# Linear attention and a tanh-shrink MLP on one core: the opening reordered around the reciprocal, a split k load, paired column tiles, and later slots for batches 1 and 2

## Chip, core and metric

The kernel runs on one core of a Trainium2 chip. The metric is device time in microseconds (us) of one execution; the time before is the median of three runs, 284.05 us (283.96 to 284.33). In what follows PE is TensorE, PEld its weight loads, DVE is VectorE, ACT is ScalarE, POOL is GpSimd, SP is SyncE. POOL and SP issue the DMA transfers: POOL those that load inputs and weights, SP stores, small transfers by way of DRAM, and a transposing DMA. "L304" is line 304 of the kernel before.

## What is computed

```python
# q, k, v: (8 batches, 8 heads, 576 positions, 64); w_in: (512, 2048); w_out: (2048, 512)
phi = lambda x: np.where(x > 0, x, np.exp(x) - 1.0) + 1.0
q_p, k_p = phi(q), phi(k)
kv  = einsum('bhsd,bhse->bhde', k_p, v);   z = k_p.sum(axis=2)
num = einsum('bhsd,bhde->bhse', q_p, kv)
den = einsum('bhsd,bhd->bhs', q_p, z)[..., None] + 1e-06
x   = (num / den).transpose(0, 2, 1, 3).reshape(8 * 576, 512)
h   = x @ w_in
out = (h - tanh(h)) @ w_out            # (4608, 512), float32
```

## The kernel before, in words

**The two halves.** The attention gives x, kept transposed in SBUF as `xT` (feature pairs p = 0 to 3 of 128 rows, all 4608 tokens). The MLP runs over nine chunks c of 512 tokens. Of each chunk the first layer (products at L430, `l1mm`) makes 16 column tiles `fi` of 128 hidden features, four products each, one for each p; ACT takes tanh and DVE subtracts (`l1act` one tile, L441 and L442; `l1act2` two tiles at once, L436 and L437) into `gT`. The second layer (L451, `l2mm`) runs in 16 slots `s` of four products, and ACT evacuates its sums (`evac`, L462), SP stores them (L475). A batch has 576 tokens, so chunk c needs batches up to c; the attention of batch c+1 and c+2 is woven into chunk c by hand. The lists `s1[fi]` and `s2[s]` hold what is emitted after column tile fi of the first layer and after slot s of the second. Within one engine the instructions run in the order in which they are emitted, so a place in such a list sets a place in each engine's queue.

**PSUM.** The 8 banks of 2 KiB a partition are one tensor, `ps_all`. In chunk 0 the column tiles use banks 4, 5, 6, 7, 0, 1, 2, 3 in turn, the first four tiles banks 0 to 3; in later chunks tile fi uses bank fi mod 6, so tile 6 has to wait until tile 0's subtraction has read its bank, tile 8 until tile 2's has.

**The opening** (batch 0, before any chunk). q, k and v of batch 0 arrive in two transfers each (`load` with halves: i = 0, 1 is the half of the heads' positions on the partitions), cast to bf16. `phi_pieces` makes phi as min(exp(x), max(x,0)+1): exp on ACT (L136, L133 for the second half of k, which goes head by head), r and the min on DVE (L137/L134, L138/L135). `a_qT_pe` transposes q on PE (L166), copies on ACT (L170) and DVE (L172). `spin(n)` multiplies zeros while PE waits. `b0_z` (L252) sums k for z, `b0_zc` (L256) puts it into `kz`, `b0_kv` (L263) makes kv, `b0_kz` (L267) copies it, `a_den` (L333, L337) makes denominators in bank 4, and one reciprocal (L346) of 128x144 columns gives `rden`. `b0_num` (L273) makes the numerators, `b0_evac` (L293, ACT) takes them out. `b0_spread` (L300) spreads the first 128 columns of `rden` over all rows by 16 fp32 products into banks 4 to 7 (32 records in the trace), and `b0_scale` (L304, DVE, eight pieces) multiplies the two into `xT`. The last 16 columns go by way of DRAM (`spread_rest`, SP, L313 and L316). Then chunk 0's first four column tiles run (L686), 256 tokens at a time.

**Batches 1 and 2.** In chunk 0, slot s2[8] holds `kv1`, s2[9] denominators, numerators and `a_split` of batch 1, s2[12] `spread1` (L419, then the scales L423 on DVE), and s2[11], s2[13] and s2[15] the exp and min pieces of batch 2's q and, at s2[15], the transposing DMA of it (L155), the stores of chunk 0 (`later`) and the r pieces of k. In chunk 1, s1[8] holds `kv2`, and s1[12] the denominators of batch 2 (`a_den`: L337, L342, L346) with `a_spread`: four small DRAM writes `ds` (L366) and two broadcasts `rdb` (L369, 576 KB each), all on SP. `a_num` at s2[12] of chunk 1 makes the numerators and `num_scale` (L401, four pieces) reads `rdb`. POOL's `gate` (L447) holds the loads of batch 3 back until batch 2's transposing DMA is through.

Of the kernel before, what the change touches and what calls it, by code (L numbers as in the profile page):

```python
# [18 lines left out]
def kernel(  # L19
# [9 lines left out]
    nc = tc.nc  # L29
# [54 lines left out]
    def load(b, t, src, halves):  # L84

        x = src[b].rearrange("h (p j) d -> (h p) (j d)", j=J)
        if halves:
            for i in range(2):
                nc.gpsimd.dma_start(out=t[:, :, i].rearrange("q h j d -> q h (j d)"),  # L89
                                    in_=x.rearrange("(h i q) x -> i q h x", h=2, i=2)[i])  # L90
        else:
            nc.gpsimd.dma_start(out=t.rearrange("q h i j d -> q (h i) (j d)"),  # L92
                                in_=x.rearrange("(n q) x -> q n x", n=4))
# [50 lines left out]
    def a_kphi(b, i):  # L144
        phi(b, k_t, kp_t, "kp", i)
# [4 lines left out]
    def new_qT(b):  # L150
        qT_t[b] = work.tile([128, 2, J, 2, 64], BF16, name="qT")
# [4 lines left out]
            out=qT_t[b].rearrange("p i j g t -> p (i j) (g t)"),  # L156
            in_=qp_t[b].rearrange("p i j h d -> p (i j h d)"))

    def a_qT_pe(b, i, banks, on=None):
        if i == 0:  # L160
            new_qT(b)
        for n in range(2):
            j0, j1 = ((0, 5), (5, 9))[n]
            ps = banks().bitcast(BF16).rearrange("p (j t) -> p j t", t=128)
            for j in range(j0, j1):
                nc.tensor.transpose(ps[:, j - j0, :], qp_t[b][:, i, j].rearrange("p h d -> p (h d)"), ident)  # L166
            src = ps[:, 0:j1 - j0, :]
            dst = qT_t[b][:, i, j0:j1].rearrange("p j g t -> p j (g t)")
            if (on or "AV")[n] == "A":
                nc.scalar.copy(dst, src)  # L170
            else:
                nc.vector.tensor_copy(dst, src)  # L172

    def quads():

# [88 lines left out]
                                 v_b[0][rs, h, i, j, :], start=(j == 0), stop=(j == J - 1))  # L264

    def b0_kz(i):
        (nc.scalar.copy if i else nc.vector.tensor_copy)(kz_t[0][:, :, i, 0:64], ps_all[:, 2 * i:2 * i + 2, 0:64])  # L267

    def num_mm(b, i, bank_of):

# [57 lines left out]
    def a_den(b, bank, parts=range(4)):  # L328

        kz, qT = kz_t[b], qT_t[b]  # L330
        ps = ps_all[:, bank, 0:J * 16]
        for t in range(4) if b == 0 else ():
            nc.tensor.matmul(ps[32 * t:32 * t + 32], eps[:, 0:32], one[:, 0:J * 16], start=True, stop=False)  # L333
        for n, p in enumerate((0, 2, 1, 3)):
            if n in parts:
                for t in range(4):
                    nc.tensor.matmul(ps[32 * t:32 * t + 32], kz[:, p // 2, p % 2, 64:96],  # L337
                                     qT[:, p % 2, :, p // 2, 16 * t:16 * t + 16],
                                     start=(n == 0 and b > 0), stop=(n == NP - 1))
        if b > 0:  # L340
            den = rpool.tile([128, J * 16], F32, name="den")
            nc.vector.tensor_scalar(den, ps, 1e-6, None, ALU.add)  # L342
        else:
            den = ps
        rden = rpool.tile([128, J * 16], F32, name="rden")
        nc.vector.reciprocal(rden, den)  # L346
        rden_t[b] = rden

    def a_split(b):
# [187 lines left out]
    for f in (eq0, rq0, mq0, eq1, rq1, mq1):  # L537
        f()
    spin(18)
    a_qT_pe(0, 0, side, "AV")  # L540
    (ek0, rk0, mk0), (ek1, rk1, mk1) = (phi_pieces(0, k_t, kp_t, "kp", i, 2 * i) for i in range(2))
    for f in (ek0, rk0):
        f()
    spin(5)
    a_qT_pe(0, 1, side, "AV")
    for f in (*ek1, mk0, rk1):
        f()
    spin(6)
    b0_z(0)
    spin(3)  # L550
    for f in mk1:
        f()
    b0_zc(0)
    b0_kv(0)
    b0_z(1)
    b0_zc(1)
    b0_kz(0)
    a_den(0, 4)
    ns0 = new_ns(0)
    spread_rest(0)  # L560
    b0_num(0)
    b0_kv(1)
    b0_kz(1)
    b0_evac(0, ns0)
    b0_num(1)
    b0_evac(1, ns0)
    b0_spread((0, 2, 1, 3), 0)
    for x in range(2):
        for n, p in enumerate((0, 2, 1, 3)):
            b0_scale(p, ns0, n, 4 * x, 4 * x + 4)  # L570

    def prepare():

# [12 lines left out]
    for c in range(NC):  # L586
# [4 lines left out]
        if c == 0:  # L591
            sub = {}

            def spread1():
                a_spread_pe(1, range(NP))
                for p in range(NP):
                    a_scale(1, p, sub["ns"], p)

            def kv1():
                a_kv(1, 4)  # L600
                pss = rest_mm(0, 4, 256)
                a_kz(1, 4)
                scale_rest(0, pss)

            def num1():
                ns = sub["ns"] = new_ns(1)
                for i in (1, 0):
                    b0 = 4 + 2 * i
                    num_mm(1, i, lambda h: b0 + h)
                    nc.scalar.copy(ns[:, i::2, 0:8, :].rearrange("p a j t -> p a (j t)"), ps_all[:, b0:b0 + 2, :])  # L610

            s2[0].append(lambda: a_qphi(1, 0))
            s2[1].append(lambda: a_qphi(1, 1))
            s2[4].append(lambda: a_kphi(1, 0))
            s2[5].append(lambda: (a_qT_pe(1, 0, Banks([4, 5])), a_qT_pe(1, 1, Banks([6, 7])), a_kphi(1, 1),
                                  load_q(2), load_k(2), load_v(2)))
            s2[2].append(prepare)
            s2[8].append(kv1)
            s2[9].append(lambda: (a_den(1, 4), num1(), spread_rest(1), a_split(1)))
            s2[12].append(spread1)  # L620

            qs, ks = [], []

            def exp2(pieces, src, store, name, i):
                pieces.append(phi_pieces(2, src, store, name, i))
                pieces[i][0]()

            def rest2(f):
                f[1]()
                f[2]()  # L630

            def k2(i):
                ks.append(phi_pieces(2, k_t, kp_t, "kp", i))
                ks[i][1]()

            s2[11].append(lambda: exp2(qs, q_t, qp_t, "qp", 0))
            s2[13].append(lambda: (rest2(qs[0]), exp2(qs, q_t, qp_t, "qp", 1)))
            s2[15].append(lambda: (rest2(qs[1]), a_qT_dma(2), [f() for f in later], k2(0), k2(1)))
        elif n1 < B:
            if c == 1:  # L640
                def kv2():
                    kv_cols_mm(2, 6, 0)
                    pss = rest_mm(1, 6, 256)
                    kz_copy(2, 6, 0)
                    scale_rest(1, pss)

                s1[8].append(kv2)
            if n1 < QS:
                s1[12].append(lambda: (a_den(n1, 6), a_spread(n1)))
            else:  # L650
                if c == 2:
                    s1[2].append(lambda: (q_den(n1, 0, 0), q_den(n1, 0, 1)))
                e = 2 * (c == 2)
                s1[3 + e].append(lambda: q_den(n1, 1, 0))
                s1[5 + e].append(lambda: q_den(n1, 1, 1))
                s1[7 + e].append(lambda: q_scale(n1))
            m = 12 if c == 1 else 9
            s2[m].append(lambda: a_num(n1, n2 if n2 < B else 0))
            if n2 < B:
                s2[m + 2].append(lambda: (q_zb(n2, 4 if c == 1 else 7), q_prod(n2)))  # L660
                if c > 1:
                    s2[15].append(lambda: (q_den(n2, 0, 0), q_den(n2, 0, 1)))
# [15 lines left out]
        if c == 0:  # L678

            first = Banks([4, 5, 6, 7, 0, 1, 2, 3])  # L680
            hs = [ps_all[:, n, :] for n in range(4)]
            for x in range(2):
                xs = slice(256 * x, 256 * x + 256)
                for n, p in enumerate((0, 2, 1, 3)):
                    for fi in range(4):
                        nc.tensor.matmul(hs[fi][:, xs], w_in_sb[:, p, fi * 128:(fi + 1) * 128], xT[:, p, xs],  # L686
                                         start=(x == 0 and n == 0), stop=(x == 1 and n == 3))
            for fi in range(4):
                l1act(fi, hs[fi], gT)
        for fi in range(4 if c == 0 else 0, NF):  # L690
            h = first() if c == 0 else ps_all[:, fi % 6, :]
            if c == 2 and fi == 1:

                for two in (0, 2):
                    for f, o in ((0, ps_all[:, 0, :]), (1, h)):
                        for p in (two, two + 1):
                            l1mm(c, f, o, p, p)
            elif c != 2 or fi > 1:
                for p in range(NP):
                    l1mm(c, fi, h, p, p)  # L700
            if c == 0:
                l1act(fi, h, gT)
            elif fi % 2:
                n = fi % 6
                l1act2(fi - 1, ps_all[:, n - 1:n + 1, :], gT)
            for f in s1[fi]:
                f()
# [56 lines left out]
```

## Time and profile before

| what | value |
|---|---|
| median of three runs | 284.05 us (283.96 to 284.33) |
| the profiled execution, its own time | 284.32 us |
| its span, first to last instruction | 282.6 us |
| PE busy in the span | 277.0 us, 98% |
| DVE, ACT, POOL busy | 176.1, 145.6, 77.5 us |
| granted TensorE clock | 1.000 |
| first product of chunk 0 (L686), first of L430 | 16.82 us, 20.30 us |
| mean of one L430 product, recorded | 379 ns (they overlap; 36 of them follow each other in 7.77 us) |

A timeline line gives start, duration, engine, line, operation, output and inputs, how many instructions are merged in it, and in brackets the idle time ahead of it with what ended it. The chain of work that ended last is followed back from the last instruction, at each step to what released it. Times of a record include its way through the engine's pipeline, so records in a row overlap by some 0.07 us on DVE.

### The profile page before, as it was taken

What the parts mean: (1) busy time and instruction counts of PE and PEld (TensorE: products, weight loads), DVE (VectorE), ACT (ScalarE), POOL (GpSimd) and SP (SyncE); (2) the same over time, 40 slices, a digit from 0 to 9 for tenths busy, and PEclk for the clock granted to TensorE, in tenths of its full rate; (3) what the DMA queues carried; (4) which work ended last, traced back from release to release, by engine and by line L of the source; (5) the groups of instructions that cost most, each with busy time, mean ns of one, the idle gap of its engine ahead of it and who ended that gap; (6) DMA issues with size and microseconds to landing.
All of it is one profiled execution on the core that took longest, in us unless ns stands there. A gap on an engine that the chain in (4) does not pass through costs nothing.

```text
span 282.6 us, 5093 instructions
## 1 busy us (share of the span) xinstructions
PE 277.0 (98%) x2084; PEld 131.9 (47%) x2084; DVE 176.1 (62%) x283; ACT 145.6 (52%) x176; POOL 77.5 (27%) x69
## 2 busy tenths in 40 slices
PE   8989999999999999999999999999999999999995
PEld 3564454454444454445444444444444444444443
DVE  5859977984779773977397639764870167006600
ACT  3648647946346753566366735572651365126411
POOL 8653120430361526233614360506050000000000
PEclk9999999999999999999999999999999999999999
DMA  6999999899994399049903792252115210230032
GB/s 103 199 207 212 205 207 209 172 192 197 236 237 76 71 194 217 5 84 162 220 22 73 115 240 60 48 110 48 29 22 123 58 32 2 57 79 13 2 74 75
DMA packets 38743, 33.12 MB, mean 117 GB/s; under 512 B 16160, under 2 KB 34624, under 8 KB 38592
## 3 DMA queue, kind: packets, MB, share of 16 engines
q0 software_dynamic: 17504, 18.35, 40.1%
q1 hardware_dynamic: 21216, 14.45, 21.8%
q8 instruction: 16, 0.26, 0.3%
q14 instruction: 7, 0.06, 0.1%
HBM read 38.14 MB, written 9.46 MB: 168 GB/s over the span
## 4 chain that ended last, share of the span: by engine, by line
PE 90%; DMA 5%; POOL 1%; ACT 1%; issue 1%; SPq 0%; DVE 0%; DVEq 0%; POOLq 0%
PE ps_all L430 43%; PE ps_all L451 41%; DMA v<-in_v_dram 3%; DMA out_dram<-osb 3%; PE ps_all L184 2%; PE ps_all L273 2%; PE ps_all L686 1%; ACT osb L462 1%; SPq L475 0%; POOL kraw L89 0%; PE ps_all L337 0%; POOL qraw L89 0%; PE ps_all L300 0%; PE ps_all L166 0%; PE ps_all L263 0%
## 5 line engine op out<-in xcount | busy, mean ns | idle before, releaser
L451 PE MATMUL ps_all<-w_out_sb,gT 128*128 128x512 bf16 x560 | 124.6, 379 | 0.0
L430 PE MATMUL ps_all<-xT,w_in_sb 128*128 128x512 bf16 x560 | 122.7, 379 | 0.0
L437 DVE TENSOR_TENSOR gT<-ps_all,th 128x1024 bf16<-128x1024 f32 x64 | 77.8, 1218 | 46.4 <-ACT th L436 46.4
L436 ACT ACTIVATE th<-ps_all 128x1024 f32<-128x1024 f32 x64 | 65.5, 1024 | 46.9 <-PE ps_all L430 46.9
L430 PEld LDWEIGHTS <-w_in_sb 128*128 128x128 bf16 x560 | 54.6, 98 | 65.5
L451 PEld LDWEIGHTS <-gT 128*128 128x128 bf16 x560 | 53.8, 98 | 63.2 <-issue 0.2
L462 ACT COPY osb<-ps_all 128x512 f32<-128x512 f32 (+1 forms) x36 | 20.7, 582 | 56.4 <-PE ps_all L451 40.0
L245 POOL TENSOR_TENSOR qp<-qp,rd 128x1152 bf16<-128x1152 bf16 x10 | 21.0, 2118 | 39.1 <-issue 23.7
L231 POOL TENSOR_TENSOR pr<-qp,zb 128x1152 f32<-128x1152 bf16 x10 | 23.5, 2362 | 21.6 <-ACT zb L224 21.6
L236 DVE TENSOR_REDUCE dn<-pr 128x9 f32<-128x576 f32 x20 | 14.5, 745 | 12.2 <-POOL pr L231 12.2
L136 ACT ACTIVATE e<-qraw 128x1152 bf16<-128x1152 bf16 x16 | 18.5, 1161 | 5.4 <-DMA qraw<-in_q_dram 5.4
L136 ACT ACTIVATE e<-kraw 128x1152 bf16<-128x1152 bf16 x15 | 17.4, 1162 | 1.9 <-DMA kraw<-in_k_dram 1.9
L138 DVE TENSOR_TENSOR qp<-e,r 128x1152 bf16<-128x1152 bf16 x16 | 12.1, 759 | 4.4 <-ACT e L136 3.3
L92 POOL DMA_DIRECT2D kraw<-in_k_dram x7 | 5.4, 769 | 33.1 <-DVE r L137 17.7
L138 DVE TENSOR_TENSOR kp<-e,r 128x1152 bf16<-128x1152 bf16 x15 | 11.4, 763 | 4.4 <-ACT e L136 3.5
L441 ACT ACTIVATE th<-ps_all 128x512 f32<-128x512 f32 x16 | 9.4, 597 | 5.5 <-PE ps_all L686 3.7
L442 DVE TENSOR_TENSOR gT<-ps_all,th 128x512 bf16<-128x512 f32 x16 | 10.4, 687 | 2.7 <-ACT th L441 1.7
L532 PE MATMUL ps_all<-zero 128*128 128x512 bf16 x32 | 10.1, 475 | 1.2 <-DVE zero L485 1.2
L92 POOL DMA_DIRECT2D qraw<-in_q_dram x7 | 5.2, 741 | 16.7 <-ACT e L136 7.3
L137 DVE TENSOR_SCALAR r<-qraw 128x1152 bf16<-128x1152 bf16 x16 | 7.4, 465 | 0.4 <-DMA qraw<-in_q_dram 0.4
L460 DVE COPY osb<-ps_all 128x128 f32<-128x128 f32 x1 | 0.3, 292 | 11.6 <-DMA out_dram<-osb 11.6
L199 DVE COPY vp<-v 128x1152 bf16<-128x1152 bf16 x10 | 5.3, 525 | 3.2 <-DMA v<-in_v_dram 3.2
(105 smaller groups left out, 141.1 us busy)
## 6 DMA issues: line engine op xcount, KB each, us to landing
out_dram<-osb SPq DMA_DIRECT2D x62, 128.0 KB, 2.5
qraw<-in_q_dram POOLq DMA_DIRECT2D x7, 576.0 KB, 10.5
kraw<-in_k_dram POOLq DMA_DIRECT2D x7, 576.0 KB, 7.8
v<-in_v_dram POOLq DMA_DIRECT2D x6, 576.0 KB, 11.4
w_in_sb<-in_moe_w_in_dram POOLq DMA_DIRECT2D x3, 512.0 KB, 13.1
w_out_sb<-in_moe_w_out_dram POOLq DMA_DIRECT2D x3, 512.0 KB, 16.3
v<-in_v_dram POOLq DMA_DIRECT2D x4, 288.0 KB, 12.9
rdb<-ds SPq DMA_DIRECT2D x2, 576.0 KB
```

Of the source, the lines that this page charges most:

```text
L92: nc.gpsimd.dma_start(out=t.rearrange("q h i j d -> q (h i) (j d)"), in_=x.rearrange("(n q) x -> q n x", n=4))
L136: return (lambda: nc.scalar.activation(e, x, AF.Exp), lambda: nc.vector.tensor_scalar(r, x, 0.0, 1.0, ALU.max, ALU.add), lambda: nc.vector ...
L138: lambda: nc.vector.tensor_tensor(y, e, r, ALU.min))
L231: nc.gpsimd.tensor_mul(pr_t[b][:, i].rearrange("p j h d -> p j (h d)"), qp_t[b][:, i].rearrange("p j h d -> p j (h d)"), zb_t[b][:, i].uns ...
L236: nc.vector.tensor_reduce(dn_t[b][:, i, :, h], pr_t[b][:, i, :, h, :], mybir.AxisListType.X, ALU.add)
L245: nc.gpsimd.tensor_mul(x, x, rd[:, i].unsqueeze(2).to_broadcast([128, J * 2, D]))
L430: nc.tensor.matmul(h, w_in_sb[:, p, fi * 128:(fi + 1) * 128], xT[:, p, c * 512:(c + 1) * 512], start=(n == 0), stop=(n == NP - 1))
L436: nc.scalar.activation(th, h, AF.Tanh)
L437: nc.vector.tensor_sub(gT[:, fi:fi + 2, :], h, th)
L442: nc.vector.tensor_sub(gT[:, fi, :], h, th)
L451: nc.tensor.matmul(o, gT[:, fi, i * 128:(i + 1) * 128], w_out_sb[:, fi, :], start=(fi == 0), stop=(fi == NF - 1))
L462: nc.scalar.copy(osb[:, f0:f1], o[:, f0:f1])
```

## The change

It does these things:
- the second part of batch 0's k is loaded in two transfers, one for each head of a pair;
- in the opening the copy of the second q half on ACT comes after both exp halves of k, z(1) ahead of kv(0), `kz` of half 0 is copied by ACT and that of half 1 by DVE, two spin products fewer;
- batch 0's reciprocal is two instructions, of 128 and 16 columns; the spread comes ahead of the second numerators, the rest's DMAs behind them in emission;
- the scales and the first four column tiles go by the pairs of i = 0 first, then i = 1; two column tiles share two banks, and tanh and subtraction take two tiles at a time;
- batch 1's slots go from s2[8], [9], [12] to [9], [10], [13]; batch 2's q exp from [11], [13] to [13], [14], its min pieces all to [15];
- in chunk 1 `kv2` goes from s1[8] to [9], the denominators of batch 2 from s1[12] to [13]; column tiles 0 and 1 of chunk 1 are interleaved as those of chunk 2 were.

```diff
         if halves:
+            y = x.rearrange("(h i q) x -> i q h x", h=2, i=2)
             for i in range(2):
-                nc.gpsimd.dma_start(out=t[:, :, i].rearrange("q h j d -> q h (j d)"),
-                                    in_=x.rearrange("(h i q) x -> i q h x", h=2, i=2)[i])
+                for hs in ((0, 1), (1, 2)) if i and src is k and b == 0 else ((0, 2),):
+                    nc.gpsimd.dma_start(out=t[:, hs[0]:hs[1], i].rearrange("q h j d -> q h (j d)"),
+                                        in_=y[i, :, hs[0]:hs[1]])
...
     def b0_kz(i):
-        (nc.scalar.copy if i else nc.vector.tensor_copy)(kz_t[0][:, :, i, 0:64], ps_all[:, 2 * i:2 * i + 2, 0:64])
+        (nc.vector.tensor_copy if i else nc.scalar.copy)(kz_t[0][:, :, i, 0:64], ps_all[:, 2 * i:2 * i + 2, 0:64])
...
-        nc.vector.reciprocal(rden, den)
+        for x in (slice(0, 128), slice(128, 144)) if b == 0 else (slice(0, 144),):
+            nc.vector.reciprocal(rden[:, x], den[:, x])
...
-    spin(5)
-    a_qT_pe(0, 1, side, "AV")
-    for f in (*ek1, mk0, rk1):
+    spin(4)
+    t1a, t1v = a_qT_pe(0, 1, side)
+    for f in (t1v, *ek1, t1a, mk0, rk1, *mk1):
         f()
     spin(6)
     b0_z(0)
-    spin(3)
-    for f in mk1:
-        f()
+    spin(2)
     b0_zc(0)
+    b0_z(1)
     b0_kv(0)
-    b0_z(1)
+    b0_kz(0)
     b0_zc(1)
-    b0_kz(0)
     a_den(0, 4)
     ns0 = new_ns(0)
-    spread_rest(0)
     b0_num(0)
+    b0_evac(0, ns0)
     b0_kv(1)
     b0_kz(1)
-    b0_evac(0, ns0)
+    spread_rest(0)
+    b0_spread((0, 2, 1, 3), 0)
     b0_num(1)
     b0_evac(1, ns0)
-    b0_spread((0, 2, 1, 3), 0)
-    for x in range(2):
-        for n, p in enumerate((0, 2, 1, 3)):
-            b0_scale(p, ns0, n, 4 * x, 4 * x + 4)
+    for i in range(2):
+        for x in range(2):
+            for n, p in ((2 * i, i), (2 * i + 1, 2 + i)):
+                b0_scale(p, ns0, n, 4 * x, 4 * x + 4)
...
-            s2[8].append(kv1)
-            s2[9].append(lambda: (a_den(1, 4), num1(), spread_rest(1), a_split(1)))
-            s2[12].append(spread1)
+            s2[9].append(kv1)
+            s2[10].append(lambda: (a_den(1, 4), num1(), spread_rest(1), a_split(1)))
+            s2[13].append(spread1)
...
-            s2[11].append(lambda: exp2(qs, q_t, qp_t, "qp", 0))
-            s2[13].append(lambda: (rest2(qs[0]), exp2(qs, q_t, qp_t, "qp", 1)))
-            s2[15].append(lambda: (rest2(qs[1]), a_qT_dma(2), [f() for f in later], k2(0), k2(1)))
+            s2[13].append(lambda: exp2(qs, q_t, qp_t, "qp", 0))
+            s2[14].append(lambda: exp2(qs, q_t, qp_t, "qp", 1))
+            s2[15].append(lambda: (rest2(qs[0]), rest2(qs[1]), a_qT_dma(2), [f() for f in later], k2(0), k2(1)))
...
-                s1[8].append(kv2)
+                s1[9].append(kv2)
             if n1 < QS:
-                s1[12].append(lambda: (a_den(n1, 6), a_spread(n1)))
+                s1[13].append(lambda: (a_den(n1, 6), a_spread(n1)))
...
-            hs = [ps_all[:, n, :] for n in range(4)]
-            for x in range(2):
-                xs = slice(256 * x, 256 * x + 256)
-                for n, p in enumerate((0, 2, 1, 3)):
-                    for fi in range(4):
-                        nc.tensor.matmul(hs[fi][:, xs], w_in_sb[:, p, fi * 128:(fi + 1) * 128], xT[:, p, xs],
-                                         start=(x == 0 and n == 0), stop=(x == 1 and n == 3))
-            for fi in range(4):
-                l1act(fi, hs[fi], gT)
+            hs = [ps_all[:, fi // 2:4:2, 256 * (fi % 2):256 * (fi % 2) + 256] for fi in range(4)]
+            for i in range(2):
+                for x in range(2):
+                    xs = slice(256 * x, 256 * x + 256)
+                    for f0 in (0, 2):
+                        for p in (i, i + 2):
+                            for fi in (f0, f0 + 1):
+                                nc.tensor.matmul(hs[fi][:, x, :], w_in_sb[:, p, fi * 128:(fi + 1) * 128], xT[:, p, xs],
+                                                 start=(p == 0 and fi == f0), stop=(p == 3 and fi > f0))
+            for n in range(2):
...
-            if c == 2 and fi == 1:
+            if c in (1, 2) and fi == 1:
...
-            elif c != 2 or fi > 1:
+            elif c not in (1, 2) or fi > 1:
```

More of the change, by code (lines that the diff above doesn't have):

```diff
@@ L157, in a_qT_dma, with a_qT_pe @@
             in_=qp_t[b].rearrange("p i j h d -> p (i j h d)"))
-    def a_qT_pe(b, i, banks, on=None):
+    def a_qT_pe(b, i, banks, on="AV"):
         if i == 0:
             new_qT(b)
+        copies = []
         for n in range(2):
@@ L168, in a_qT_pe @@
             dst = qT_t[b][:, i, j0:j1].rearrange("p j g t -> p j (g t)")
[L169 to L172, printed above, removed]
+            copies.append((nc.scalar.copy if on[n] == "A" else nc.vector.tensor_copy, dst, src))
+        return [lambda f=f, d=d, x=x: f(d, x) for f, d, x in copies]
     def quads():
@@ L539 @@
     spin(18)
-    a_qT_pe(0, 0, side, "AV")
+    for f in a_qT_pe(0, 0, side):
+        f()
     (ek0, rk0, mk0), (ek1, rk1, mk1) = (phi_pieces(0, k_t, kp_t, "kp", i, 2 * i) for i in range(2))
@@ L614 @@
             s2[4].append(lambda: a_kphi(1, 0))
[L615 removed]
+            s2[5].append(lambda: ([f() for i in range(2) for f in a_qT_pe(1, i, Banks([4 + 2 * i, 5 + 2 * i]))], a_kphi(1, 1),
                                   load_q(2), load_k(2), load_v(2)))
             s2[2].append(prepare)
[L618 to L620 removed]
+            s2[9].append(kv1)
+            s2[10].append(lambda: (a_den(1, 4), num1(), spread_rest(1), a_split(1)))
+            s2[13].append(spread1)
             qs, ks = [], []
@@ L680 @@
             first = Banks([4, 5, 6, 7, 0, 1, 2, 3])
-            hs = [ps_all[:, n, :] for n in range(4)]
-            for x in range(2):
-                xs = slice(256 * x, 256 * x + 256)
-                for n, p in enumerate((0, 2, 1, 3)):
-                    for fi in range(4):
-                        nc.tensor.matmul(hs[fi][:, xs], w_in_sb[:, p, fi * 128:(fi + 1) * 128], xT[:, p, xs],
-                                         start=(x == 0 and n == 0), stop=(x == 1 and n == 3))
-            for fi in range(4):
-                l1act(fi, hs[fi], gT)
+            hs = [ps_all[:, fi // 2:4:2, 256 * (fi % 2):256 * (fi % 2) + 256] for fi in range(4)]
[8 more added lines that the diff above has]
+            for n in range(2):
+                th = mpool.tile([128, 2, 512], F32, name="th")
+                h = ps_all[:, n:4:2, :]
+                nc.scalar.activation(th, h, AF.Tanh)
+                nc.vector.tensor_sub(*(y.rearrange("p x (f t) -> p f x t", f=2) if i else
+                                       y.rearrange("p f (x t) -> p f x t", x=2)
+                                       for i, y in enumerate((gT[:, 2 * n:2 * n + 2, :], h, th))))
         for fi in range(4 if c == 0 else 0, NF):
             h = first() if c == 0 else ps_all[:, fi % 6, :]
-            if c == 2 and fi == 1:
+            if c in (1, 2) and fi == 1:
                 for two in (0, 2):
```

## The prediction

> **What bounds the kernel now.** I read the page first (busy shares, then the chain that ended last), then the chain in order of time, then the timelines of TensorE (PE), VectorE (DVE) and the DMA queue SP around the places that the change touches.
>
> ```profile
> PE 277.0 (98%) x2084; PEld 131.9 (47%) x2084; DVE 176.1 (62%) x283; ACT 145.6 (52%) x176; POOL 77.5 (27%) x69
> PE 90%; DMA 5%; POOL 1%; ACT 1%; issue 1%; SPq 0%; DVE 0%; DVEq 0%; POOLq 0%
> ```
> ```profile
> 4.80 7.41 DMA v<-in_v_dram
> ...
> 14.37 0.27 ACT kz L267
> ...
> 14.69 0.41 PE ps_all L273 x4
> 15.10 1.15 PE ps_all L300 x32
> ...
> 16.34 0.43 DVE xT L304
> ...
> 16.82 3.65 PE ps_all L686 x32
> 20.47 10.36 PE ps_all L430 x48
> ```
> TensorE is the bound: once the first real product starts at 16.82 us it is never idle for long until the stores at 269 us. So three things can move the time: when the product at 16.82 starts, TensorE's own work (the change adds and removes no product outside the opening), and new waits of TensorE later. Three spots of other engines decide those waits:
>
> ```profile
> 46.16 2.48 DVE L423 TENSOR_TENSOR xT<-ns,ps_all 128x512 bf16<-128x512 f32 x4 [1.18 <-PE ps_all L419]
> ...
> 51.76 1.22 DVE L437 TENSOR_TENSOR gT<-ps_all,th 128x1024 bf16<-128x1024 f32 x1
> ...
> 53.67 1.21 DVE L437 TENSOR_TENSOR gT<-ps_all,th 128x1024 bf16<-128x1024 f32 x1
> ```
> ```profile
> 62.60 1.05 DVE L346 RECIPROCAL rden<-den 128x144 f32<-128x144 f32 x1
> 63.57 1.16 DVE L437 TENSOR_TENSOR gT<-ps_all,th 128x1024 bf16<-128x1024 f32 x1
> ```
> ```profile
> 68.75 1.12 SPq L369 DMA_DIRECT2D rdb<-ds  x2
> ```
> ```profile
> L401 DVE TENSOR_TENSOR xT<-ps_all,rdb x4: 681/681/681, 77.3 to 79.1; 128x512 bf16<-128x512 f32 x4
> L401 DVEq EVENT_SEMAPHORE  x1: 21/21/21, 77.1 to 77.1; - x1
> ```
> Between 46.16 and 57.95 DVE has no idle row: its queue is full. And the last line shows batch 2's scale (L401) standing at 77.1 at a wait for the broadcast rdb; the landing events of the second broadcast end at 77.08. It has about 0.15 us to spare, since DVE is busy until 77.37 anyway.
>
> **The opening.** Before: both `min` halves of k (L135) end at 12.62; the second one waits for the second `Exp` half (ACT to 12.12), whose first half could start only when all of k's second part had landed (10.8). With h=0 in a transfer of its own, that first `Exp` is done before; the second runs 10.87 to 11.54 (0.67, row L133), and DVE runs r (0.45) and both halves (0.46, then 0.38 after overlap) back to back from the landing: 12.25, a gain of 0.37. The moved ACT copy t1a (0.68) then ends at 12.2, before its reader at 13.2. On PE, z(1) now goes ahead of kv(0): kv(0) (0.28 of starts) lay in the shadow of that wait and now lies on the path, so the last L337 ends at 13.45 instead of 13.68. kz of half 0 goes from DVE to ACT (0.28 to 0.27) and is done at 13.4, before num(0) needs it. Spins of zeros (two fewer matmuls) fill waits only.
>
> The reciprocal in two: the rows 128x144 (1053 ns) and 128x36 (378 ns) give 6.25 ns a column and 0.15 fixed, so 0.95 and 0.25, some 0.08 of it overlapped. It starts at 13.49 instead of 13.73 and ends at 14.62 instead of 14.79. The spread (L300) is now ahead of num(1), which held it from 14.84 to 15.03; it starts at 14.68, ends 0.35 earlier, and the first scale goes from 16.34 to 15.99, the first product from 16.82 to 16.46. Does the spread wait for both pieces? In before, the first L304 reads columns 0 to 63 of the four banks, which the spread's first four products write, yet starts after the last of the 32 at 16.25: waits go by whole PSUM banks. The spread writes the bank that both pieces read, so I take both; released by the first piece alone it would start 0.19 earlier.
>
> The Trainium skill (PSUM — Partial Sum Buffer, "PSUM bank collisions raise a hardware error") asks for guards by bank even where columns differ, so it too speaks against the split: by it the split costs about 0.1 (a second fixed cost), by column-wise guards it brings the 0.19.
>
> The L686 block: products go by pairs of i, 0.109 each. The second scale comes 0.34 after the first, two products fill 0.22, so 0.12 of wait; the evacuation of i=1 (1.03, now after num(1)) ends at 17.2, before banks 2 and 3 are needed at 17.4; i=1's scales (17.3 to 18.8) keep ahead. The full-width L430 start goes from 20.30 to 20.07: **-0.23**.
>
> The third k transfer is one more issue on POOL (0.72 by its rows), ahead of v and the weights. Their transfers are queued: issues 0.72 apart land about 1.45 apart, v issued at 4.80 lands at 12.2. So I cost the slot at nothing; without that cover v and w_in come 0.72 later. Ends: -0.5 (spread released early, k's second piece a little earlier) to +0.5 (second piece 0.7 late).
>
> The Trainium skill (DMA: Bandwidth & Descriptors, "Anatomy of one DMA — SWDGE (gpsimd) path") gives about 2.0 us fixed per transfer; paid in series this would turn -0.23 into about +1.8. The rows' 1.45 spacing shows that it is overlapped.
>
> **First four column tiles by pairs.** Two tanh of 1.02 and two subtractions of 1.22 take the place of four of 0.60 and 0.69; banks 0 to 3 are free again at 22.1 and 23.3 for products at 23.5 and later. Zero; were this late, each bank would cost its lateness.
>
> **Slots of batch 1 (0.86 us later each).** kv, den and num move with equal distance; their inputs (v of batch 1 landed by 39.6) only get older: zero. The spread L419 moves from 45.63 to 46.49 in PE's own time, so L423 starts at 47.02, not 46.16, and everything queued behind it on DVE with no idle time is 0.86 later: the four q pieces, two k pieces, and the first L437s. xT's pairs 2 and 3 are ready at 49.0 and 49.6; the interleaved first two column tiles of c=1 want them at 49.43 and 49.64: covered; without the interleave 0.35. The first L437 then ends at 53.84 (52.98+0.86), but column tile 6 wants its bank at 48.57+24x0.2158 (7.77/36, the chain's row of L430) = 53.75: wait 0.15 with 0.055 of hand-over. The second ends at 55.74, tile 8 wants its bank at 55.47+0.15: another 0.18. Together **+0.32**; ends 0 (DVE recovers) and 0.6.
>
> Also behind those q pieces: the transposing DMA (SP, 2.83) and eight stores, later by 0.86-0.23 = 0.63, and POOL's gate (L447), which holds back the loads of batch 3: its v lands at 71.1 instead of 70.5, the vp and kp pieces behind it end at 73.7, two us before PE reads them. The stores and qT's readers have over 3 us. ACT's two moved `Exp` have data (q of batch 2 landed 46.3) and free banks in time.
>
> **Slots of batch 2.** kv2 one tile later: inside slack. The denominators move from after tile 12 to after tile 13, and so behind the L437 of tiles 12/13 in DVE's queue. In PE's time the tile-13 products end at 61.75, tanh 61.8 to 62.8, L437 to 64.1, den 0.30, reciprocal to 65.4, where it was 63.65: +1.74, not one slot. With PE itself at +0.09 (-0.23+0.32) that is +1.83 for what hangs on it: the four ds writes, the wait until 68.75 for their landing, the two 576 KB broadcasts. Their data ran after v of batch 3 had landed (70.5), on an otherwise empty software queue, so they gain nothing by starting later: landing 78.9. L401 starts at 79.0 (was 77.29); its fourth piece ends 2.48 later, 81.5. PE wants pair 3 at 80.13+0.09. Wait: 81.5+0.05-80.22 = **+1.3**. Ends: 0.4, if the reciprocal moves by the slot alone (0.86); 1.6, if the stores interleave worse. Nothing gives this back: later stages are full of PE.
>
> **Sum:** -0.23+0.32+1.3 = +1.4. The profiled execution took 284.32 (span 282.6 and 1.7 around), 0.27 over the median; it would become 285.7, the median 285.45.
>
> **Rivals.**
> A, the forecast, +0.9 to +1.7. For it: the wait row at 77.1 and the queue order. 70%.
> B, the broadcast is hidden: it lands by 78.0, DVE is ready then and stage c=2 waits 0.3 or less. Sum -0.23+0.32+0.2 = +0.3, 284.35. For it: it ran beside 8 stores and a k load, so some of its 8.3 us may be contention. Against: the ds writes themselves take the 3.4 us from 64.96 at the last issue. 17%.
> C, faster: the opening gains 0.5 or more and the DVE queue does not hold PE, since the spread is released by the first piece of the reciprocal and the interleaved order hides the late scales; with both later waits at zero, -0.5 to -0.7, 283.4. It decides if the broadcast lands before 77.7. Against: the full DVE rows after 46.16. 7%.
> D, the k pieces: the extra issue delays v, w_in and what follows by its 0.72 on top of A, 286.1. 6%.
>
> **How the numbers follow.** 0.2%, 0.57 us, is about what a measurement of this kernel can tell from no change: 283.48 and 284.62 are the bounds. Faster: C and a little of B, 0.08. Same: B and A's lowest part, 0.18. Slower 0.74. The range from 284.1 to 286.0 leaves out C, half of D and B's low end; A alone is 284.95 to 285.75.
>
> **What would show it.** First L686 near 16.46 and L430 near 20.07. PE waits for L437 of about 0.15 each at tiles 6 and 8 of c=1. L346 of batch 2 near 64.4 to 65.5, after the L437 of tiles 12/13. The waits of TensorE should then list xT from the L401 line near 80 with about 1 us. Wrong if that wait is absent, or if the broadcast lands before 78.

## The result and the profile after

The changed kernel takes 286.59 us (median of 6 runs, 286.27 to 287.76); the kernel before took 284.19 beside it (6 runs, 283.96 to 284.87). The ratio is 1.0086, with a 95% interval from 1.0065 to 1.0107: slower, as forecast, but by 2.4 us where the sum had 1.4, and 0.6 above the upper end of the range. The profiled execution took 286.76 with a span of 285.0 (before 282.6), at a granted clock of 1.0 in both, so the spans can be laid side by side. One execution of the kernel before (487 us) and one of `e6_slots_pairs` (484 us) ran at 0.56 of the clock and are left out of the medians and ratios below. In line numbers, L686 of before is now L690, L430 is L432, L437 is L439, L441/L442 are L443/L444, L138 is L140, L199 is L200, L346 is L348, L401 is L403, L423 is L425, L369 is L371, L300 is L301, L184 is L185; of k's second half in the opening, r is L136 (L134) and the min L137 (L135); the pairs of the first four tiles are L695 (tanh) and L696 (subtraction).

The busy shares and the chain that ended last, page of the changed kernel:

```profile
PE 277.6 (97%) x2082; PEld 131.7 (46%) x2082; DVE 176.7 (62%) x282; ACT 145.4 (51%) x174; POOL 77.8 (27%) x70
PE 82%; DMA 8%; DVE 5%; issue 1%; ACT 1%; SPq 1%; POOL 0%; DVEq 0%; POOLq 0%
```

The busy time of every engine is the same to 0.6 us; what has changed is who ends last. TensorE's part of the chain has fallen from 90% to 82%. The chain in order of time of the same run says where the others have come in (start, duration, what):

```profile
10.82 0.65 DVE r L136
11.57 0.84 DVE kp L137 x2
13.72 1.08 DVE rden L348 x2
14.84 1.22 PE ps_all L301 x32
16.63 3.76 PE ps_all L690 x32
...
53.84 1.65 DVE kp L140
55.49 1.15 DVE gT L439
56.68 1.89 PE ps_all L432 x8
...
65.61 1.06 DVE rden L348
67.69 4.10 DMA ds<-rden
71.80 0.48 SPq L371
72.33 7.59 DMA rdb<-ds
80.01 2.50 DVE xT L403 x4
```

Before, hardly anything but TensorE stood in the chain between 16.82 and 269 us. Now there are two breaks: a piece of batch 2's k (kp, L140) that takes 1.65 us in chunk 1, and the way from batch 2's reciprocal by way of DRAM to the scales of chunk 2. The waits of TensorE name the same two (us in total, times, longest):

```profile
PE ps_all L432 <- DVE gT L439: 0.8, 1, 0.8
...
PE ps_all L432 <- DVE xT L403: 0.6, 3, 0.2
```

That view counts idle time after the modelled end of the pipeline. Measured from one product's start to the next, less the usual 0.216 us, the stalls after 16.6 us are: 0.16 at column tile 9 of chunk 0, 0.15 at tile 6 and 0.98 at tile 8 of chunk 1, and 0.41, 0.38 and 0.34 at the first products of chunk 2. With the first L432 at 20.23 instead of 20.30 this gives -0.07+0.16+0.15+0.98+1.13 = +2.35, against +2.4 between the spans; another 0.08 lies inside kv of batch 2 in chunk 1.

**The break in chunk 1.** VectorE's timeline of the changed kernel and its kp row in the kernel before, then GpSimd's of the changed kernel, then GpSimd's of the kernel before (start, duration, engine, line, operation, how many merged, idle time ahead):

```profile
47.10 2.48 DVE L425 TENSOR_TENSOR xT<-ns,ps_all 128x512 bf16<-128x512 f32 x4 [1.19 <-PE ps_all L421]
...
52.71 1.22 DVE L439 TENSOR_TENSOR gT<-ps_all,th 128x1024 bf16<-128x1024 f32 x1
53.84 1.65 DVE L140 TENSOR_TENSOR kp<-e,r 128x1152 bf16<-128x1152 bf16 x1
55.41 1.21 DVE L439 TENSOR_TENSOR gT<-ps_all,th 128x1024 bf16<-128x1024 f32 x1
```
```profile
52.90 0.85 DVE L138 TENSOR_TENSOR kp<-e,r 128x1152 bf16<-128x1152 bf16 x1
```
```profile
52.50 2.38 POOL L200 COPY vp<-v 128x1152 bf16<-128x1152 bf16 x2 [10.64 <-DMA v<-in_v_dram]
```
```profile
51.99 2.76 POOL L199 COPY vp<-v 128x1152 bf16<-128x1152 bf16 x2 [11.08 <-DMA v<-in_v_dram]
```

The same kp piece takes 0.76 us elsewhere and took 0.85 at this place before. It has two bf16 inputs in SBUF; GpSimd at that time copies v of batch 2 in two pieces. In the changed kernel the second copy runs from 53.74 to 54.88; kp starts 0.10 after the copy's start, and ends 0.61 after its end. Before, kp started at 52.90, 0.24 before the first copy's end, and again ended 0.61 after it; there kp went next, and it was the second copy that took 1.68 instead of 1.14. So the two take turns: whoever comes second stands until the other's instruction is through. The Trainium skill (SBUF — State Buffer, "Who interferes with whom") says this: a VectorE instruction with two SBUF inputs contends with a GpSimd instruction that reads SBUF, and the first to start holds the port to its end. Both orders of this pair of traces agree with it (1.65 for the one, 1.68 for the other).

**The break at chunk 2.** SP's and VectorE's timelines of the changed kernel, to be read against 68.75 (SP) and the last row here (VectorE) of the kernel before:

```profile
71.80 1.12 SPq L371 DMA_DIRECT2D rdb<-ds  x2
```
```profile
65.61 1.05 DVE L348 RECIPROCAL rden<-den 128x144 f32<-128x144 f32 x1
...
80.01 2.48 DVE L403 TENSOR_TENSOR xT<-ps_all,rdb 128x512 bf16<-128x512 f32 x4 [1.37 <-DMA rdb<-ds]
```
```profile
77.29 2.48 DVE L401 TENSOR_TENSOR xT<-ps_all,rdb 128x512 bf16<-128x512 f32 x4
```

VectorE now idles for 1.37 us until the broadcast lands. The reciprocal is 3.0 later than before: 1.3 that TensorE is late by then, and 1.7 of its own.

**The pairs.** ScalarE's timeline of the changed kernel:

```profile
19.99 1.02 ACT L695 ACTIVATE th<-ps_all 128x1024 f32<-128x1024 f32 x1 [2.57 <-PE ps_all L690]
22.37 1.02 ACT L695 ACTIVATE th<-ps_all 128x1024 f32<-128x1024 f32 x1 [1.35 <-DVE gT L696]
```

The second tanh (banks 1 and 3) waits for the first subtraction (banks 0 and 2), although they share no bank. VectorE then runs 0.95 late through chunk 0: batch 1's q pieces start at 33.05 instead of 32.10.

### The profile page after: what moved, and what is told of

It is laid out like the page before. It is cut to its first block, busy times and chain, and to the rows that moved or that the text cites. A ratio compares the mean times of both kernels' runs of the same rounds, so it can differ in the third digit from the quotient of the medians.

```text
span 285.0 us, 5087 instructions
## 1 busy us (share of the span) xinstructions
PE 277.6 (97%) x2082; PEld 131.7 (46%) x2082; DVE 176.7 (62%) x282; ACT 145.4 (51%) x174; POOL 77.8 (27%) x70
## 4 chain that ended last, share of the span: by engine, by line
PE 82%; DMA 8%; DVE 5%; issue 1%; ACT 1%; SPq 1%; POOL 0%; DVEq 0%; POOLq 0%
PE ps_all L432 40%; PE ps_all L453 35%; DMA rdb<-ds 3%; DMA out_dram<-osb 2%; DMA qraw<-in_q_dram 2%; PE ps_all L185 2%; DMA ds<-rden 1%; PE ps_all L690 1%; PE ps_all L274 1%; DVE xT L403 1%; ACT e L138 1%; DVE rden L348 1%; DVE gT L439 1%; ACT osb L464 1%; DVE kp L140 1%
## 5 line engine op out<-in xcount | busy, mean ns | idle before, releaser
L432 PE MATMUL ps_all<-xT,w_in_sb 128*128 128x512 bf16 x560 | 123.5, 379 | 1.5 <-DVE gT L439 0.8
L439 DVE TENSOR_TENSOR gT<-ps_all,th 128x1024 bf16<-128x1024 f32 x64 | 77.7, 1217 | 45.9 <-ACT th L438 45.8
L432 PEld LDWEIGHTS <-w_in_sb 128*128 128x128 bf16 x560 | 54.6, 98 | 68.0 <-issue 3.1
L138 ACT ACTIVATE e<-qraw 128x1152 bf16<-128x1152 bf16 x16 | 18.5, 1161 | 3.6 <-DMA qraw<-in_q_dram 3.6
L138 ACT ACTIVATE e<-kraw 128x1152 bf16<-128x1152 bf16 x15 | 17.4, 1162 | 1.0 <-DMA kraw<-in_k_dram 1.0
L140 DVE TENSOR_TENSOR kp<-e,r 128x1152 bf16<-128x1152 bf16 x15 | 12.2, 815 | 4.4 <-ACT e L138 3.5
L140 DVE TENSOR_TENSOR qp<-e,r 128x1152 bf16<-128x1152 bf16 x16 | 12.1, 758 | 4.4 <-ACT e L138 3.5
L444 DVE TENSOR_TENSOR gT<-ps_all,th 128x512 bf16<-128x512 f32 x12 | 7.8, 686 | 0.8
L443 ACT ACTIVATE th<-ps_all 128x512 f32<-128x512 f32 x12 | 7.2, 597 | 2.0 <-DVE gT L444 1.1
L200 DVE COPY vp<-v 128x1152 bf16<-128x1152 bf16 x10 | 5.2, 524 | 2.7 <-DMA v<-in_v_dram 2.7
```

The source lines that it names most:

```text
L138: return (lambda: nc.scalar.activation(e, x, AF.Exp), lambda: nc.vector.tensor_scalar(r, x, 0.0, 1.0, ALU.max, ALU.add), lambda: nc.vector ...
L140: lambda: nc.vector.tensor_tensor(y, e, r, ALU.min))
L432: nc.tensor.matmul(h, w_in_sb[:, p, fi * 128:(fi + 1) * 128], xT[:, p, c * 512:(c + 1) * 512], start=(n == 0), stop=(n == NP - 1))
L439: nc.vector.tensor_sub(gT[:, fi:fi + 2, :], h, th)
```

## The experiments

Every run has the kernel before beside it on the same chip, and each ratio is to it; its medians there were 284.43 (`e1` to `e4`), 284.33 (`e5` to `e8`) and 284.36 (`e9` to `e11`). The changed kernel was timed only beside the 284.19 above, so a distance from its 286.59 also holds the 0.14 to 0.24 us between those medians.

**Both sets of slots back.** `e1_slots_back`, the changed kernel with

```diff
-            s2[9].append(kv1)
+            s2[8].append(kv1)
-            s2[10].append(lambda: (a_den(1, 4), num1(), spread_rest(1), a_split(1)))
+            s2[9].append(lambda: (a_den(1, 4), num1(), spread_rest(1), a_split(1)))
-            s2[13].append(spread1)
+            s2[12].append(spread1)
...
-                s1[13].append(lambda: (a_den(n1, 6), a_spread(n1)))
+                s1[12].append(lambda: (a_den(n1, 6), a_spread(n1)))
```

and q's pieces of batch 2 and `kv2` back likewise.

> The changed kernel with the slots of batches 1 and 2 as in the kernel before; opening, pairs and interleave stay. Theory A (the time went to late queues of VectorE: 1.13 us of waits in chunk 1 and 1.13 us at the start of chunk 2): both go, 284.2 to 284.5 us. Rival B (the paired tiles and the split k load cost more than the trace's 0.16 us at tile 9, by way of VectorE being 0.95 us later in chunk 0): the time stays above 285.3.

Measured: 285.25 us, ratio 1.0029 (1.0019 to 1.0039); between the theories. The stalls at chunk 2 are gone, but 0.8 stays, and a wait has come that the changed kernel does not have:

```profile
PE ps_all L185 <- DVE kp L140: 0.5, 1, 0.5
```

That is kv of batch 1, which at its old slot meets the VectorE that the pairs have made late (0.62 from start to start, with 0.16 at tile 9 and 0.26 at tile 8 of chunk 1). So the pairs are not free; in the changed kernel the later slot of kv hides most of their cost. The old slots don't keep kp away from GpSimd's copy either: with TensorE and VectorE late by then for these reasons, kp starts at 53.84 and takes 1.65 here too.

**Only the denominators of batch 2 back.** `e2_den_back`, the changed kernel with the last two lines of the diff above alone.

> The changed kernel with batch 2's denominators back after column tile 12 of chunk 1. Theory A (the reciprocal stands behind the subtraction of tiles 12/13, everything up to the broadcast hangs on it): reciprocal 1.8 us earlier, broadcast landed by 78.2, the 1.13 us of waits at chunk 2's start gone, 1.1 us less than the changed kernel. Rival B (the broadcast lands late because its transfers collide with the stores, whenever they start): the landing moves by less than 0.9 and 0.5 us or more of wait stay.

Measured: 285.43, ratio 1.0036 (1.0025 to 1.0048), 1.16 below the changed kernel (1.4 by the distances from the kernel before, 1.0 against 2.4). The reciprocal starts at 63.68, the scales at 78.39 with no idle time ahead, and chunk 2 starts without a wait; the waits in chunk 1 stay (0.14 and 0.98). The term of batch 2's slot is shown.

**The same from the other side.** `e7_den_later_alone`, the kernel before with this one line changed the other way (s1[12] to s1[13]).

> The kernel before with one edit: the denominators and reciprocal of batch 2 in chunk 1 go from s1[12] to s1[13]. Theory A (the reciprocal then stands behind the subtraction of tiles 12 and 13, and the broadcast lands later by as much): reciprocal of batch 2 at about 64.4 instead of 62.60, the scales L401 about 1.2 to 1.8 later than 77.29, waits of TensorE in sum 0.6 to 1.3 at the start of chunk 2: 285.0 to 285.6. Theory B (it costs only on top of a chunk 1 that is late already): under 284.7.

Measured: 285.60, ratio 1.0046 (1.0030 to 1.0062), that is +1.27. VectorE's timeline of this run:

```profile
64.20 1.05 DVE L346 RECIPROCAL rden<-den 128x144 f32<-128x144 f32 x1
78.82 2.48 DVE L401 TENSOR_TENSOR xT<-ps_all,rdb 128x512 bf16<-128x512 f32 x4 [1.56 <-DMA rdb<-ds]
```

One slot later costs 1.6 us at the reciprocal, because it gets behind the subtraction of tiles 12 and 13, and 1.35 at TensorE (0.63+0.38+0.33). Theory A: the edit costs as much where chunk 1 is on time.

**The kp pieces out of the way.** `e3_kp_later`, the changed kernel with

```diff
-                s1[1 + 2 * i].append(lambda i=i: (ks[i][0](), ks[i][2]()))
+                s1[3 + 2 * i].append(lambda i=i: (ks[i][0](), ks[i][2]()))
```

> The changed kernel with batch 2's k pieces (exp and min) two column tiles later, so the subtraction of tiles 2/3 goes ahead of the first min. Theory A (the min, two bf16 operands in SBUF, was held until GpSimd's copy of v ended at 54.88, and the subtraction stood behind it): first min at its usual 0.76, wait at tile 8 gone, wait at tile 6 0.15 as before, about 1.0 us less than the changed kernel. Rival B (VectorE is slow in that stretch for another reason): the subtraction of tiles 2/3 or the min is stretched in its new place too, gain below 0.5.

Measured: 286.07 (285.34 to 287.03), ratio 1.0068 (1.0049 to 1.0088). In the profiled run, 285.34, kp starts behind both copies and takes its usual time, and the 0.98 at tile 8 is gone:

```profile
54.64 0.75 DVE L140 TENSOR_TENSOR kp<-e,r 128x1152 bf16<-128x1152 bf16 x1
```

The 1.2 at chunk 2 stays. The trace is that of theory A, but the median is only 0.5 below the changed kernel, where 1.0 was expected. The four times scatter by 1.7 us; what the longer ones met isn't shown, since only one execution was profiled.

**v's copies on VectorE.** `e4_vp_dve`, the changed kernel with

```diff
-            s1[0].append(lambda: (a_vp(2, 0, nc.gpsimd), a_vp(2, 1, nc.gpsimd),
-                                  gate(qT_t[n1]), load_k(n2), load_q(n2), load_v(n2)))
+            s1[5].append(lambda: (a_vp(2, 0), a_vp(2, 1)))
+            s1[0].append(lambda: (gate(qT_t[n1]), load_k(n2), load_q(n2), load_v(n2)))
```

> The changed kernel with batch 2's two copies of v done by VectorE after tile 5, none by GpSimd. Theory A (shared access of VectorE and GpSimd to SBUF): the first min takes 0.76 again, the wait at tile 8 falls from 0.98 to 0.18, 0.7 to 0.8 us less than the changed kernel. Rival B (the transposing DMA, issued at 52.1, slows the min): the min stays at 1.6 and the time does not fall.

Measured: 286.43, ratio 1.0070 (1.0055 to 1.0085): hardly below the changed kernel. The first kp takes 0.75 with no copy on GpSimd, and tile 8 waits only 0.08. The time goes elsewhere: kv of batch 2 now waits 0.35 for vp, and the stall at chunk 2 is 1.35, which take back 0.57 of the 0.90. In the profiled run, the slowest of the four at 286.86, the opening was also 0.6 later (first L432 at 20.84 instead of 20.23), which this edit doesn't touch. So the mechanism is confirmed and the transposing DMA is ruled out, and as a repair the edit gains little.

**The pairs in neighbouring banks.** `e5_pairs_next`, the changed kernel with

```diff
-            hs = [ps_all[:, fi // 2:4:2, 256 * (fi % 2):256 * (fi % 2) + 256] for fi in range(4)]
+            hs = [ps_all[:, fi - fi % 2:fi - fi % 2 + 2, 256 * (fi % 2):256 * (fi % 2) + 256] for fi in range(4)]
...
-                h = ps_all[:, n:4:2, :]
+                h = ps_all[:, 2 * n:2 * n + 2, :]
```

> The changed kernel with one edit: the two column tiles of a pair lie in neighbouring banks (0 and 1, then 2 and 3) and not in every second one (0 and 2, then 1 and 3). Same number and size of instructions. Theory A (the wait of ACT's second tanh for the first subtraction comes from the overlapping stretches of banks): the second tanh starts about 21.1 instead of 22.37, the second subtraction ends near 23.4 instead of 24.65, the wait of 0.16 at column tile 9 is gone, and the q pieces of batch 1 start on DVE about 1.1 earlier (near 31.9). The later waits (0.98 at tile 8 of chunk 1, 1.1 at the start of chunk 2) stay, so 0.1 to 0.3 us less than the changed kernel: 286.3 to 286.5. Theory B (the tanh waits for the banks it shares with something else, or for its buffer): the second tanh stays at 22.4 and nothing moves.

Measured: 286.52, ratio 1.0076 (1.0060 to 1.0092). The two subtractions now follow each other (21.37 to 23.73) and the wait at tile 9 is gone, so the overlap of the strided stretches made the tanh wait (whether the chip asks for that or only the program's own guards isn't shown). The total is what was expected only because its parts cancel. Products now write bank 2 earlier, while the second numerators are still being read from it, and the L690 block has 0.30 more of wait. And in chunk 1 the collision has moved to another victim, VectorE's timeline and the wait behind it:

```profile
52.14 2.72 DVE L139 TENSOR_SCALAR r<-kraw 128x1152 bf16<-128x1152 bf16 x2
```
```profile
PE ps_all L432 <- DVE gT L439: 1.9, 1, 1.9
```

GpSimd's copies started at 51.99 in this run, and both r pieces of k (one SBUF input, usually 0.45) take 1.40 behind them. TensorE waits 2.0 at tile 6, and not at all at the start of chunk 2. TensorE's lateness alone doesn't explain that, for the reciprocal hangs on it and comes 1.0 later too (66.63). But the broadcast was issued 3.7 us after the first ds write, where the other twelve profiles have 5.0 to 5.3. With 5.1 it would have landed some 1.4 later, and the stall would have been about that of the changed kernel (an estimate: the changed kernel's 8.2 from this issue to the scales puts them at 81.0 with the first product wanted at 81.36, against 80.01 and 80.35 there). What shortened the way in this run isn't shown.

**Slots back and neighbouring banks.** `e6_slots_pairs`, both edits together.

> The changed kernel with the slots of batches 1 and 2 as before, and the pairs in neighbouring banks. Theory A (the 0.9 us by which the run with the old slots alone stood over the kernel before were the pairs' 0.95 us of lateness on DVE, paid as 0.16 at tile 9, 0.62 at kv of batch 1 and 0.26 at tile 8 of chunk 1): these waits go, and the time is within 0.4 of the kernel before, 284.0 to 284.8. Theory B (the rest of the change, the opening above all, costs by itself): it stays at 285.0 or more.

Measured: 284.59, ratio 1.0008 (0.9998 to 1.0018). Without the pairs' lateness the waits at tile 9 and at kv are gone; 0.26 at tile 8 of chunk 1 (kp again 1.66) and the 0.30 in the L690 block stay. Theory A.

**The third k transfer undone.** `e8_k_two`, the changed kernel with

```diff
-                for hs in ((0, 1), (1, 2)) if i and src is k and b == 0 else ((0, 2),):
+                for hs in ((0, 2),):
```

> The changed kernel with the second part of batch 0's k in one transfer again. Theory A (the third transfer frees only one of the two exponentials, and the r that bounds the chain then runs beside POOL's next issue at 0.64 instead of 0.45): time within 0.3 of the changed kernel, first product of chunk 0 between 16.6 and 16.9. Theory B (the third transfer is what brings the opening forward): first product 0.3 or more later, 17.0 or more, and 0.3 us or more over the changed kernel. Theory C (the extra issue costs v and the weights 0.7): 0.3 us or more under it.

Measured: 286.43, ratio 1.0072 (1.0054 to 1.0090); first L690 at 16.64 (changed kernel 16.63). Theory A: within 0.2 of the changed kernel, neither gain nor cost can be seen. In this profile all of k's second part had landed at 10.19 (before 10.78), so the r piece, which ended at 11.48, set the chain even with one transfer; what the split is worth when k lands late isn't shown.

**The later slots of batch 1 alone.** `e10_b1_alone`, the kernel before with kv, denominators and spread of batch 1 one slot later and the interleave of chunk 1:

```diff
-            s2[12].append(spread1)
+            s2[13].append(spread1)
...
-            if c == 2 and fi == 1:
+            if c in (1, 2) and fi == 1:
```

> The kernel before with two edits of the change: kv, denominators and spread of batch 1 at s2[9], [10], [13], and the first two column tiles of chunk 1 interleaved. Theory A (the kp piece of DVE, 0.86 later, now arrives while POOL's second vp copy holds what both need, and takes about 1.6 us instead of 0.85): a wait of TensorE of 0.5 to 1.0 at column tile 8 of chunk 1, 0.1 to 0.2 at tile 6: 284.9 to 285.5. Theory B (the lateness on DVE passes on and no more, as the sum of the prediction had it): 0.3 in all, 284.5 to 284.75, the kp piece at 0.85 or less.

Measured: 285.39, ratio 1.0032 (1.0020 to 1.0044), +1.03. Theory A in its cause and its size, though not in its place: the scales L423 start at 46.98 (before 46.16, as forecast), and here it is the second r piece of k that meets the copies, so the wait of TensorE (1.09) is at tile 6:

```profile
51.84 1.80 DVE L137 TENSOR_SCALAR r<-kraw 128x1152 bf16<-128x1152 bf16 x2
53.56 1.21 DVE L437 TENSOR_TENSOR gT<-ps_all,th 128x1024 bf16<-128x1024 f32 x1
```

**Slots back, tanh by token halves.** `e9_halves_slots`, the slots as in `e1_slots_back`: the products write the banks of the changed kernel, and the pairs are taken as banks 0 and 1, then 2 and 3, which is the order in which they are done.

```diff
-                h = ps_all[:, n:4:2, :]
+                h = ps_all[:, 2 * n:2 * n + 2, :]
...
+                nc.vector.tensor_sub(*(y.rearrange("p k (f t) -> p (k f) t", f=2) if i else y
+                                       for i, y in enumerate((gT[:, 0:4, 256 * n:256 * n + 256], h, th))))
```

> The changed kernel with the slots of batches 1 and 2 as before, and tanh and subtraction of the first four column tiles taken by token halves: banks 0 and 1 (tokens 0 to 255 of all four tiles), then banks 2 and 3, which are neighbours and complete in this order; the products are written as in the changed kernel. Theory A (the pairs' lateness on DVE comes from the banks that the two tanh share, and neighbours in other positions cost 0.3 in the opening only because bank 2 is still being read there): no wait at tile 9, kv of batch 1 or tile 8 of chunk 1 beyond 0.3 in sum, no added 0.3 in the L690 block, DVE at the q pieces of batch 1 at 32.1 or earlier: 283.9 to 284.4, at or under the kernel before. Theory B (the opening or the pairs cost by themselves): 284.6 or more.

Measured: 284.16 (11 runs, 283.93 to 284.77) against 284.36 (22 runs), ratio 0.9994 (0.9986 to 1.0003): the opening and the pairs without their costs are level with the kernel before. ScalarE's timeline of this run:

```profile
19.52 1.94 ACT L695 ACTIVATE th<-ps_all 128x1024 f32<-128x1024 f32 x2 [2.14 <-PE ps_all L690]
```

Both tanh run back to back, and TensorE has no stall over 0.05 from 17 us to the end of chunk 2's first tiles. It is the best of the versions, and no measurable gain. The meeting with GpSimd is there as well (kp takes 1.27 at 52.78), but VectorE is early enough for it to cost TensorE nothing.

**Three repairs in the changed kernel.** `e11_three_mended`: denominators back, kp later, tanh by token halves, everything else of the change kept.

> The changed kernel with its three costs mended and everything else kept, batch 1's later slots too: the denominators of batch 2 back at s1[12], the kp pieces of batch 2 two column tiles later (s1[3], s1[5]), the first four tiles by token halves. Theory A (these three are the whole loss): waits of TensorE in chunks 0 to 2 at most 0.3 in sum, 284.1 to 284.6. Theory B (a fourth cost, in the later slots of batch 1 or elsewhere): 284.9 or more, and a wait in the list that none of the earlier runs had.

Measured: 285.18, but from 284.02 to 287.10 in ten runs, ratio 1.0030 (1.0009 to 1.0050). The profiled run, 284.04, is theory A: 0.14 at tile 6 is its only stall after 17 us. Four of the ten lie at 284.0 to 284.4, the others from 285.1 up, and none of those was profiled. With the later slots of batch 1 and the later kp pieces (the two runs that have both scatter most, this one by 3.1 and `e3_kp_later` by 1.7; the changed kernel's own six times span 1.5) the time hangs on something that varies from execution to execution. That GpSimd's copies, which start when v lands, meet VectorE at a different place each time would fit; it isn't shown.

## Why the prediction was right and wrong

**Slots of batch 2, +1.3: right.** The reciprocal did go behind the subtraction of tiles 12 and 13, the broadcast did land at about 80, and TensorE stalled 1.13 there; alone the edit costs +1.27, undone it gives back 1.2 to 1.4. The idle note of the timeline at L403 (1.37 until rdb) is the one that was named. Rival B is out: the scales moved by 2.72; TensorE's own lateness by then accounts for 1.3 of it and the slack that the scales had before (the last ended at 79.77, wanted at 80.13) for 0.36, and the rest, about 1.1, is the stall.

**Slots of batch 1, +0.32: the step that failed.** The lateness of VectorE was as forecast (L425 at 47.10, forecast 47.02), and so was tile 6 (0.15 for 0.15). At tile 8 the sum had 0.18 and the run has 0.98, because the step moved a queue in time and kept every duration. The kp piece was carried over with its 0.85 of before, when its true length depends on what GpSimd does at the moment. The trace of before held the hint: that 0.85, where the same operation takes 0.76, and a GpSimd copy of 1.68 beside one of 1.14. The term is 1.13, not 0.32, and the upper end of 0.6 was too low. These +0.8 are most of the 1.0 that was missing; the opening and the pairs each add 0.16, and the slots of batch 2 came 0.17 under their term.

**Pairs, zero: wrong.** They were costed as four instructions against eight by their durations, with tanh and subtraction of different pairs overlapping. They do not overlap: 1.35 of idle time on ScalarE, a subtraction that ends at 24.65 where 23.3 was forecast, 0.16 at tile 9 of chunk 0. The 0.95 that VectorE is late from there costs little in the changed kernel, since kv of batch 1 has moved later too; with kv at its old place it cost 0.62 more. The sum treated the two edits as independent, and they are not.

**Opening, -0.23: right in its order, but the gain isn't there.** Spread behind both pieces of the reciprocal: it starts at 14.84, the second piece ends at 14.79 (the first at 14.67), so the split brings nothing, and waits go by banks as assumed. The wait inside the L690 block is 0.11 (forecast 0.12). What differs is the r piece of k's second half: 0.64 instead of 0.45, beside a DMA issue of GpSimd (10.43 to 11.18), and with it the first product at 16.63 (forecast 16.46) and the full-width start at 20.23 (forecast 20.07). In all ten profiles with the changed opening the first product came 5.16 to 5.17 after the end of this r, so r's start and length set the opening. Its start was hit by luck: the sum had r wait for k's landing at 10.8, but k's last transfer landed at 10.13, and r began at 10.82 because VectorE was in the min of the first half until then. With 0.45 (four profiles) the first product came at 16.31, 16.33, 16.43 and 16.59; over the ten it lay between 16.31 and 17.12, mean 16.64, and in the three profiles with the old opening at 16.62, 16.77 and 16.82. The forecast gain of 0.36 at this product is thus about 0.1 on average, and the wait in the L690 block takes that back. Rival C is out by the bank waits, and D by `e8_k_two` and by the landings: v came in at 11.61 and 13.02, before at 12.21 and 13.58.

## What to carry to other kernels

When a change shifts one engine's queue in time, do not carry the old durations over: list what the engines that share something with it do at the new time, first of all GpSimd copies and GpSimd DMA issues against VectorE's SBUF-to-SBUF work, and treat a row that is longer than its like as a sign of a meeting. Price a group of edits as a group, since a later slot can hide a lateness that another edit makes. When two instructions are meant to overlap on different PSUM banks, give each a stretch of neighbouring banks, in the order in which they are filled.

## What was not expected of the hardware

VectorE's r also takes turns with GpSimd's issues of DMA transfers. In the six profiles of the changed opening in which the r piece of k's second half (L136) started 0.25 to 0.49 us after an issue had begun, it ended 0.26 to 0.29 after the issue's end, and took 0.57 to 0.75 instead of 0.45. In four in which it started 0.05 to 0.10 after the issue's begin, it took 0.45, and the issue 0.81 to 0.86 where the six had 0.75 to 0.77. So an issue is not only a queue's cost: it can lengthen the operation that the chain runs through.

The way of the denominators through DRAM is not always of one length either: from the first ds write's issue to the first broadcast's issue it was 5.0 to 5.3 us in twelve profiles (5.1 in the changed kernel) and 3.7 in `e5_pairs_next`.
